# Attention with top-k and two dense layers: a DMA transposes f16 halves of the probabilities, VectorE takes more lower halves

## The chip, the cores and the metric

The kernel runs on one core of a Trainium2 chip, in one launch. The metric is the device time of a run in microseconds (us); lower is better. A core has a matrix engine (TensorE, PE in the profile; its weight loads are PEld), VectorE (DVE), ScalarE (ACT), GpSimd (POOL) and a queue engine (SP) that issues the DMAs here. PSUM is the memory into which PE writes, SBUF the working memory. Each engine takes its instructions in the order in which the program has them.

## The reference

```python
# q, k, v: (4, 8, 576, 64); 8 heads of 64 give 512 columns
scores = (1 / np.sqrt(64)) * np.matmul(q, k.transpose(0, 1, 3, 2))
kth = np.partition(scores, -32, axis=-1)[..., -32:-31]
scores = np.where(scores >= kth, scores, -1e9)
scores = scores - np.max(scores, axis=-1, keepdims=True)
attn = np.exp(scores)
attn = attn / (np.sum(attn, axis=-1, keepdims=True) + 1e-09)
x = np.matmul(attn, v)                       # as rows: (2304, 512)
gate = 1 / (1 + np.exp(-(x @ w_gate)))       # w_gate, w_val: (512, 1536)
h = (gate * (x @ w_val) @ w_out) @ w_in      # w_out: (1536, 512), w_in: (512, 1024)
e = np.exp(h - h.max(-1, keepdims=True))
solu = h * e / (e.sum(-1, keepdims=True) + 1e-9)
ln = (solu - solu.mean(-1)) / np.sqrt(solu.var(-1) + 1e-6) * g_ln
out = ln @ w_out2                            # (1024, 512)
```

## The kernel before

Attention is cut into 72 steps, 18 for each of the four batches. A step has 2 x 128 rows of scores against 576 keys: one pair of heads for 128 queries, or, for the 64 queries left over in each batch, two pairs. The steps 0 to 17 are batch 0 (`WHOLE`, kept in full f32), the others batches 1 to 3. Four steps fill one chunk of 128 rows of `x`; 18 chunks then go through the two dense layers.

A step runs as follows. PE makes the scores (`scores`, L607), ACT copies them to an `s` tile (L614), DVE folds the row's two halves into a `w` tile (L621, L625) and finds the 32 largest with MAX8 and MATCH_REPLACE8 (L635, L639). From the 32nd, DVE and POOL make a threshold (L653 to L663), ACT writes what lies below it to `w` (L668), POOL subtracts that from `s` (L672), ACT takes the exponential with the sum (L677), and DVE inverts the sum (L686). POOL scales the probabilities in place (`norm`, L694; ACT in the first six steps, L692). PE transposes the nine 128 x 128 blocks in three groups (`flip`, L704). For batch 0, ACT copies each group to SBUF (L711). For batches 1 to 3 ACT writes the upper f16 half (`take_flip`, L714), and DVE subtracts it from what PSUM holds and writes the lower half (`rest_flip`, L719). PE multiplies with V (`attend`, L738), for batches 1 to 3 in three f16 products of halves.

The dense layers also work with f16 halves. The upper half is an ACT copy. The lower half is made in one of two ways. In chunks 16 and 17 (`DIRECT`) DVE takes it from PSUM in one instruction (`lower`, L771). In the others ACT makes a second copy in full precision and POOL subtracts: rows of x (`rows_all`, L760, `rows_rest`, L777), the middle (`mid_all`, L948, `mid_rest`, L954), the turned last layer (`turn_all`, L1045, `turn_rest`, L1053).

The order of all this is made before the program is written. `Order` is a planner: each piece of work is added with its engine, a cost, a due time, what it needs, and which tiles it takes and frees. It plays the work forwards and backwards and then writes the instructions in the order found. `SHIFT` holds corrections to the due times, one number for each kind of work. `BUFS` says how many tiles of each kind there are; a tile that is not free holds back the work that takes it. The loads of K land in `s` tiles.

Of the kernel before, what the change touches and what calls it, by code (L numbers as in the profile page):

```python
# [40 lines left out]
DIRECT = (16, 17)
FULL = 2.0 ** 15

BUFS = dict(s=4, ks=8, v=4, qr=3, qs=3, w=2, et=4, eu=2, ps=1, pt=1, av=1, pm=4, xt=1, gh=1, two=3, big=2, xf=1, x2=1)
# [1161 lines left out]
```

## Time and profile before

| | |
|---|---|
| median of 3 runs | 1100.3 us (1100.17 to 1100.45) |
| profiled execution | 1101.9 us |
| its span, first to last instruction | 1100.1 us |
| busy: PE, DVE, ACT, POOL | 970.6, 971.5, 827.8, 701.2 us |
| granted TensorE clock, mean | 0.944 |

The times of engines overlap, so busy times do not add up to the span. The profile shows one execution; "idle before" is the time that an engine stood still just before an instruction, with the one that released it. PE is little used in the first 200 us, while weights are rebuilt and the first steps run; from 200 to 1000 us PE and DVE are nearly full; in the last 100 us PE finishes the last chunks and DVE is at 31%.

### The profile page before, as it was taken

To read this page: it belongs to the slowest core of one execution; us is meant where nothing else is said; L and a number is where in the kernel's file an instruction comes from. 1 tells how busy PE (TensorE), PEld (TensorE's weight loads), DVE (VectorE), ACT (ScalarE), POOL (GpSimd) and SP (SyncE) were. 2 spreads that over 40 slices of the span, in tenths; PEclk is the share of its full clock that TensorE was granted. 3 is DMA by queue.
4 is the path that set the end of the run, shared out by engine and by line. 5 is a ranking of instruction groups with operands and counts; after the bars stand their busy time and mean duration, and the time that the engine had idled before them with its cause. 6 is when DMAs were issued, how large, how long until landed. Compare 5 with 4: busy or idle time off the path is not lost.

```text
span 1100.1 us, 31341 instructions
## 1 busy us (share of the span) xinstructions
PE 970.6 (88%) x12500; PEld 801.8 (73%) x12500; DVE 971.5 (88%) x2888; ACT 827.8 (75%) x1561; POOL 701.2 (64%) x940
## 2 busy tenths in 40 slices
PE   1455747799999999999999999999999999999996
PEld 1334736589796878796978879797878798778952
DVE  7999999999698999999999999997998999893242
ACT  2698499997889787787889677778789787765431
POOL 2556378887877675878678665778678657652100
PEclk9756768899999999999999999999999999999998
DMA  9854241001220000012110000022100000000000
GB/s 318 289 162 139 85 137 69 6 21 52 75 74 12 26 12 22 26 50 64 53 33 7 26 25 8 26 64 63 53 28 22 22 11 7 12 11 11 2 11 19
DMA packets 29474, 59.16 MB, mean 54 GB/s; under 512 B 3984, under 2 KB 14224, under 8 KB 29328
## 3 DMA queue, kind: packets, MB, share of 16 engines
q1 hardware_dynamic: 29328, 57.16, 15.8%
q8 instruction: 98, 1.61, 0.6%
q14 instruction: 48, 0.39, 0.1%
HBM read 52.43 MB, written 4.72 MB: 52 GB/s over the span
## 4 chain that ended last, share of the span: by engine, by line
DVE 32%; PE 31%; ACT 20%; POOL 9%; DMA 5%; issue 3%; POOLq 0%; SPq 0%; DVEq 0%; ACTq 0%
DVE m L635 9%; DVE w L639 7%; PE px L927 6%; PE pg L881 5%; PE ph L964 4%; PE pv L881 4%; PE po L1062 4%; DVE et L719 3%; PE pt L704 3%; ACT w L668 2%; ACT s L677 2%; PE ps L607 2%; POOL s L672 2%; DVE pd L415 2%; DVE pd L411 2%
## 5 line engine op out<-in xcount | busy, mean ns | idle before, releaser
L635 DVE MAX8 m<-w 128x8 f32<-128x576 f32 (+1 forms) x576 | 340.0, 604 | 2.8
L639 DVE MATCH_REPLACE8 w<-m,w 128x288 f32<-128x288 f32 (+1 forms) x432 | 234.9, 545 | 0.0
L672 POOL TENSOR_TENSOR s<-s,w 128x576 f32<-128x576 f32 x144 | 203.2, 1420 | 37.2 <-ACT w L668 36.8
L927 PE MATMUL px<-gh,wo 128*128 128x128 f16 x2592 | 178.4, 220 | 0.0
L881 PE MATMUL pg<-xt,wg 128*128 128x128 f16 x2592 | 168.8, 221 | 8.2 <-POOL xt L777 5.9
L927 PEld LDWEIGHTS <-wo 128*128 128x128 f16 x2592 | 157.3, 98 | 22.3 <-issue 0.5
L881 PE MATMUL pv<-xt,wv 128*128 128x128 f16 x2592 | 168.7, 220 | 0.2 <-ACT xg L948 0.2
L881 PEld LDWEIGHTS <-wv 128*128 128x128 f16 x2592 | 155.3, 99 | 15.6 <-issue 0.7
L881 PEld LDWEIGHTS <-wg 128*128 128x128 f16 x2592 | 154.1, 99 | 14.5 <-issue 6.5
L607 PE MATMUL ps<-ks,qs 128*128 128x288 f32 x640 | 129.2, 330 | 31.4 <-DVE w L625 20.3
L704 PE MATMUL pt<-ident,s 128*128 128x128 f32 x648 | 117.5, 290 | 30.4 <-ACT et L711 14.2
L668 ACT ACTIVATE w<-s,ed 128x576 f32<-128x576 f32 x144 | 120.8, 869 | 25.3 <-POOL ed L663 24.3
L607 PEld LDWEIGHTS ps<-ks,qs 128*128 128x128 f32 x640 | 97.0, 200 | 46.1 <-issue 11.1
L614 ACT ACTIVATE s<-ps 128x576 f32<-128x576 f32 x144 | 93.1, 647 | 43.1 <-PE ps L607 37.4
L677 ACT ACTIVATE s<-s,nm 128x576 f32<-128x576 f32 x144 | 111.7, 776 | 16.8 <-POOL s L672 15.6
L964 PE MATMUL ph<-wi,x 128*128 128x512 f16 x432 | 121.6, 391 | 2.4 <-ACT x L944 2.4
L1062 PE MATMUL po<-wo,lt 128*128 128x512 f16 x432 | 120.5, 394 | 1.6 <-DVE sg L909 1.1
L704 PEld LDWEIGHTS pt<-ident,s 128*128 128x128 f32 x648 | 76.0, 146 | 60.0 <-ACT et L711 20.0
L714 ACT ACTIVATE et<-pt 128x512 f16<-128x512 f32 x162 | 78.9, 487 | 48.1 <-PE pt L704 47.4
L694 POOL TENSOR_SCALAR s<-s,sm 128x576 f32<-128x576 f32 x132 | 97.3, 746 | 21.7 <-DVE sm L686 19.5
L719 DVE SCALAR_TENSOR_TENSOR et<-pt,et 128x512 f16<-128x512 f32 x162 | 89.0, 549 | 18.4 <-ACT et L714 17.8
L738 PE MATMUL av<-et,v 128*64 128x128 f16 (+3 forms) x2200 | 87.0, 234 | 0.2 <-POOL v L597 0.2
(179 smaller groups left out, 1681.4 us busy)
## 6 DMA issues: line engine op xcount, KB each, us to landing
kr<-in_k_dup_dram SPq DMA_DIRECT2D x16, 576.0 KB, 4.0
qr<-in_q_main_dram SPq DMA_DIRECT2D x64, 128.0 KB, 2.4
v<-in_v_pad_dram SPq DMA_DIRECT2D x16, 320.0 KB, 4.0
wi<-in_w_gate_dram SPq DMA_DIRECT2D x8, 512.0 KB, 6.2
wo<-in_w_val_dram SPq DMA_DIRECT2D x8, 512.0 KB, 6.6
raw<-in_w_in_dram SPq DMA_DIRECT2D x8, 512.0 KB, 4.9
wi<-in_w_out_dram SPq DMA_DIRECT2D x8, 512.0 KB, 3.8
raw<-in_w_out_dram SPq DMA_DIRECT2D x8, 512.0 KB, 3.3
```

Source lines behind the costliest of these rows:

```text
L607: nc.tensor.matmul(pt[:, nn, :S // 2], qs[:, hl, slot], ks[:, nn * (S // 2):(nn + 1) * (S // 2)], start=x == 0, stop=x == len(mm) - 1)
L635: nc.vector.max(st["m8"][:, t, r * 8:r * 8 + 8], ranked(i, r, t))
L639: nc.vector.match_replace(w, steps[i]["m8"][:, t, r * 8:r * 8 + 8], w, LOW)
L668: nc.scalar.activation(st["w"][:, t], st["s"][:, t], AF.Relu, bias=st["ed"][:, 1, t:t + 1], scale=st["ed"][:, 0, t:t + 1])
L672: nc.gpsimd.tensor_sub(st["s"][:, t], st["s"][:, t], st["w"][:, t])
L677: nc.scalar.activation(w, w, AF.Exp, bias=st["nm"][:, t:t + 1], scale=D ** -0.5, accum_out=st["sm"][:, t:t + 1])
L704: nc.tensor.transpose(pt[:, x], wf[:, k * P:(k + 1) * P], ident)
L719: nc.vector.scalar_tensor_tensor(et[:, 1], st["pt", g][:, :et.shape[2]], 1.0, et[:, 0], op0=OP.mult, op1=OP.subtract)
L881: nc.tensor.matmul(dst, w[a][:, c, f * P:(f + 1) * P], ch["xt"][:, b, c], start=x == 0, stop=x == len(mm) - 1)
L927: nc.tensor.matmul(ch["px"][:, e], wo1h[a][:, f, e * P:(e + 1) * P], ch["gh"][:, b, f], start=y == 0, stop=y == len(DOWN) - 1)
L964: nc.tensor.matmul(ch["ph", nn], ch["x2"][:, a, c], wih[b][:, c, nn * 512:(nn + 1) * 512], start=c == 0 and a == 0 and b == 0, stop=c == K ...
L1062: nc.tensor.matmul(ch["po"], ch["lt"][:, a, f], wo2h[b][:, f], start=y == 0, stop=y == len(FIN) - 1)
```

## The change

For batches 1 to 3 PE no longer transposes. ACT writes the upper f16 half of the scaled probabilities from `s` into a new tile `h` (`prob_hi`), which takes a `w` tile's place. ACT (first half of the step) and POOL (second half) scale `s` in place as `norm` did, POOL subtracts the upper half and writes the lower (`prob_lo`), and one DMA on SP transposes all 18 blocks of 128 x 128 f16 into an `et` tile (`flip_halves`). `attend` reads that.

`DIRECT` now holds the chunks 4 to 17, so DVE takes the lower halves from PSUM there, with a factor for each half of a chunk that has rows of two batches (`row_factors`). What else chunks 16 and 17 did differently hangs on the new `LATE`. `BUFS` changes: `s` 4 to 3, `w` 2 to 3, `et` and `eu` to two `et` tiles. All numbers of `SHIFT` change, and with them the order; two of its lines are shown.

```diff
-DIRECT = (16, 17)
+DIRECT = tuple(range(4, 18))
+LATE = (16, 17)
-BUFS = dict(s=4, ks=8, v=4, qr=3, qs=3, w=2, et=4, eu=2, ps=1, pt=1, av=1, pm=4, xt=1, gh=1, two=3, big=2, xf=1, x2=1)
+BUFS = dict(s=3, ks=8, v=4, qr=3, qs=3, w=3, et=2, ps=1, pt=1, av=1, pm=4, xt=1, gh=1, two=3, big=2, xf=1, x2=1)
 SHIFT = {
-    ("w", "g"): -488.7, ("sw", "g"): -373.8, ("wl", "g"): -1.3, ("swl", "g"): 331.2, ("w", "v"): -152.2,
...
+    ("M", 7): -116.2, ("M", 8): 264.5, ("M", 9): -207.8, ("M", 10): -5.3, ("M", 11): -98.3, ("M", 12): -78.9,
...
 def norm(i, t):
-        if i < EARLY:
+        if i < EARLY or t == 0 and steps[i]["b"] not in WHOLE:
             nc.scalar.activation(w, w, AF.Copy, scale=st["sm"][:, t:t + 1])
...
+    def prob_hi(i, t):
+        st = steps[i]
+        if "h" not in st:
+            st["h"] = tl(sp, [P, 2, 2, S], F16, f"h{i}", "w")
+        nc.scalar.activation(st["h"][:, 0, t], st["s"][:, t], AF.Copy, scale=st["sm"][:, t:t + 1])
+
+    def prob_lo(i, t):
+        st = steps[i]
+        nc.gpsimd.tensor_sub(st["h"][:, 1, t], st["s"][:, t], st["h"][:, 0, t])
+
+    def flip_halves(i):
+        st = steps[i]
+        st["et"] = tl(sp, [P, 2, NBLK, P], F16, f"et{i}", "et")
+        nc.sync.dma_start(st["et"].rearrange("p c k q -> p (c k) q"), st["h"].rearrange("p c a b -> p (c a b)"), transpose=True)
...
-    def rest_flip(i, g):
-        st = steps[i]
-        et = st["et", g]
-        nc.vector.scalar_tensor_tensor(et[:, 1], st["pt", g][:, :et.shape[2]], 1.0, et[:, 0], op0=OP.mult, op1=OP.subtract)
...
     def rows_direct(ch):
-        lower(ch["xt"][:, 1], ch["av"], 1.0 / PROB, ch["xt"][:, 0])
+        for w, by in row_factors(ch):
+            lower(ch["xt"][:, 1, :, w], ch["av"][:, :, w], by, ch["xt"][:, 0, :, w])
...
+            for t in range(2):
+                add(("hh", i, t), "ACT", 0.67, e, lambda i=i, t=t: prob_hi(i, t), [("iv", i)] + [("hh", i, 0)] * t, take=["w"] * (t == 0))
+                add(("no", i, t), *(("ACT", 0.67) if t == 0 else ("POOL", 0.73)), e, lambda i=i, t=t: norm(i, t), [("hh", i, t)])
+                add(("hl", i, t), "POOL", 1.385, e, lambda i=i, t=t: prob_lo(i, t), [("no", i, t)] + [("hl", i, 0)] * t,
+                    free=["s"] * t)
+            add(("tr", i), "DMA", 3.5, e + 3, lambda i=i: flip_halves(i), [("hl", i, 1)], take=["et"], free=["w"], delay=1.5)
```

In the changed kernel the lines are 1 to 17 higher: the folds are L622 and L626, MAX8 L636, `norm` L693 and L695, `prob_hi` L717, `prob_lo` L721, `flip_halves` L726, `lower` L782, the first matrices' products L898, the threshold's penalty L673. The names below carry the number of the step behind the tile's letter (`w42` is the `w` tile of step 42, `m8` its 8 x 4 maxima with the step behind, `et41_0` the first group of step 41).

On DVE, in the middle of batch 2, before: the top-k work of steps 43 and 44, with lower halves of the steps 40 and 41.

```order
L719 SCALAR_TENSOR_TENSOR et40_2_10362<-pt40_2_10346,et40_2_10362 128x128
L977 TENSOR_REDUCE st_10344<-st_10344 128x1
L635 MAX m843_10173<-w43_10128 128x8
L980 TENSOR_SCALAR st_10344<-st_10344,n2_9518 128x1
L621 TENSOR_TENSOR w44_10393<-ps44_0_10365,s44_10385 128x288
L639 MATCH_REPLACE w43_10128<-m843_10173,w43_10128 128x576
L625 TENSOR_TENSOR w44_10393<-ps44_0_10365,s44_10385 128x288
L635 MAX m843_10173<-w43_10128 128x8
L996 TENSOR_SCALAR st_10344<-st_10344 128x1
L686 RECIPROCAL sm42_10158<-sm42_10158 128x2
L719 SCALAR_TENSOR_TENSOR et41_0_10419<-pt41_0_10387,et41_0_10419 128x512
```

The same place now, at the start of step 42:

```order
L782 SCALAR_TENSOR_TENSOR lt_9533<-pl_9478,lt_9533 128x512
L636 MAX m841_9438<-w41_9427 128x8
L782 SCALAR_TENSOR_TENSOR x2_9552<-px_8856,n2_9393,x2_9552 128x512
L622 TENSOR_TENSOR w42_9616<-ps42_0_9556,s42_9595 128x288
L640 MATCH_REPLACE w41_9427<-m841_9438,w41_9427 128x576
L636 MAX m842_9626<-w42_9616 128x8
L636 MAX m841_9438<-w41_9427 128x8
L640 MATCH_REPLACE w42_9616<-m842_9626,w42_9616 128x288
L782 SCALAR_TENSOR_TENSOR lt_9533<-pl_9599,lt_9533 128x512
```

The three lower halves of a step are gone; lower halves of the dense layers stand between the top-k instructions instead, four to a chunk of four steps.

On POOL, at step 42, before: subtraction, scaling, and the rows of chunk 9.

```order
L672 TENSOR_TENSOR s42_9936<-s42_9936,w42_9950 128x576
L645 TENSOR_SCALAR nm43_10304<-m843_10173 128x2
L672 TENSOR_TENSOR s42_9936<-s42_9936,w42_9950 128x576
L777 TENSOR_TENSOR xt9_10295<-xf_10309,xt9_10295 128x512
L682 TENSOR_SCALAR sm42_10158<-sm42_10158 128x2
L694 TENSOR_SCALAR s42_9936<-s42_9936,sm42_10158 128x576 x2
```

POOL at step 42 now:

```order
L673 TENSOR_TENSOR s42_9595<-s42_9595,w42_9616 128x576
L565 TENSOR_TENSOR qs46_0_9833<-qr46_0_9549,qs46_0_9833 128x256
L683 TENSOR_SCALAR sm42_9778<-sm42_9778 128x2
L663 TENSOR_TENSOR ed44_9943<-m844_9804,ed44_9943 128x2
L664 TENSOR_SCALAR ed44_9943<-ed44_9943 128x2
L673 TENSOR_TENSOR s44_9771<-s44_9771,w44_9786 128x576
L721 TENSOR_TENSOR h42_10016<-s42_9595,h42_10016 128x576
L646 TENSOR_SCALAR nm43_10105<-m843_10020 128x2
L695 TENSOR_SCALAR s42_9595<-s42_9595,sm42_9778 128x576
L673 TENSOR_TENSOR s44_9771<-s44_9771,w44_9786 128x576
L721 TENSOR_TENSOR h42_10016<-s42_9595,h42_10016 128x576
```

One scaling is gone from POOL and two subtractions (L721) have come, with the penalty of step 44 between them; the rows of the chunk are gone.

On SP, at the boundary to batch 2 (`kr2` are the loads of K of that batch), now:

```order
L726 DMA_TRANSPOSE et30_7249<-h30_7070 128x18x128
L569 DMA kr2_0_7334<-in_k_dup_dram 128x2x576
L555 DMA qr38_0_7376<-in_q_main_dram 128x256
L726 DMA_TRANSPOSE et31_7544<-h31_7339 128x18x128
L569 DMA kr2_1_7602<-in_k_dup_dram 128x2x576
L555 DMA qr39_0_7712<-in_q_main_dram 128x256
L569 DMA kr2_2_7797<-in_k_dup_dram 128x2x576
L726 DMA_TRANSPOSE et32_7819<-h32_7673 128x18x128
```

The transposing DMAs stand in one queue with the loads, one to a step; before, the queue held loads and stores alone. On PE, behind the last product of attention, there stand 51 products of the last layer (72 before), 228 of the third matrix (204), 16 transposes (24); the numbers of the other products are the same.

## Rows read from the trace of the kernel before

**Rows 1.** The page: busy time by engine, and the chain that ended last
```profile
PE 970.6 (88%) x12500; PEld 801.8 (73%) x12500; DVE 971.5 (88%) x2888; ACT 827.8 (75%) x1561; POOL 701.2 (64%) x940
...
DVE 32%; PE 31%; ACT 20%; POOL 9%; DMA 5%; issue 3%; POOLq 0%; SPq 0%; DVEq 0%; ACTq 0%
```

**Rows 2.** Busy time by stretch: start:end, length, engines, granted clock, DMA share, GB/s
```profile
200.00:300.00 100.00, 95.66 (x1165) 80.84 (x1164) 91.58 (x284) 85.83 (x164) 82.16 (x110) 0.98 0.13 38
300.00:400.00 100.00, 95.57 (x1396) 82.23 (x1394) 93.17 (x300) 87.76 (x174) 75.23 (x103) 1.00 0.11 36
...
300.00:992.00 692.00, 676.26 (x9345) 567.16 (x9343) 659.75 (x2039) 554.42 (x1081) 492.42 (x681) 1.00 0.10 31
```

**Rows 3.** The chain, 300 to 992 us, longest pieces: start, length, what
```profile
488.35 4.70 DMA kr<-in_k_dup_dram
...
736.91 3.73 DMA kr<-in_k_dup_dram
```

**Rows 4.** Groups of DVE, 300 to 992 us: busy, mean ns, idle before
```profile
L719 DVE SCALAR_TENSOR_TENSOR et<-pt,et 128x512 f16<-128x512 f32 x103 | 70.2, 681 | 6.9 <-ACT et L714 6.7
...
L719 DVE SCALAR_TENSOR_TENSOR et<-pt,et 128x128 f16<-128x128 f32 x51 | 14.5, 284 | 0.4 <-ACT et L714 0.2
```

**Rows 5.** One piece of the chain (0.60), and the timeline of DVE
```profile
614.50 0.60 DVE et L719
...
599.34 0.27 DVE L719 SCALAR_TENSOR_TENSOR et<-pt,et 128x128 f16<-128x128 f32 x1
599.53 0.14 DVE L653 TENSOR_SCALAR ed<-m 128x1 uint32<-128x1 uint32 x1
```

**Rows 6.** Timeline of PE's weight side: the transposes of one step
```profile
601.07 0.42 PEld L704 LDWEIGHTS pt<-ident,s 128*128 128x128 f32 x4
...
604.55 0.42 PEld L704 LDWEIGHTS pt<-ident,s 128*128 128x128 f32 x4
...
607.44 0.14 PEld L704 LDWEIGHTS pt<-ident,s 128*128 128x128 f32 x1
```

**Rows 7.** Groups of ACT over the whole span, by shape
```profile
L714 ACT ACTIVATE et<-pt 128x512 f16<-128x512 f32 x108 | 64.1, 593 | 39.5 <-PE pt L704 39.2
...
L1045 ACT ACTIVATE lf<-pl 128x512 f32<-128x512 f32 x32 | 19.3, 604 | 0.2 <-POOL lt L1053 0.2
...
L714 ACT ACTIVATE et<-pt 128x128 f16<-128x128 f32 x54 | 14.8, 275 | 8.6 <-PE pt L704 8.2
...
L948 ACT ACTIVATE xg<-px,n 128x512 f32<-128x512 f32 x16 | 11.2, 698 | 0.0
...
L692 ACT ACTIVATE s<-s,sm 128x576 f32<-128x576 f32 x12 | 8.7, 764 | 1.6 <-DVE sm L686 1.5
```

**Rows 8.** Groups of POOL over the whole span, by shape
```profile
L672 POOL TENSOR_TENSOR s<-s,w 128x576 f32<-128x576 f32 x144 | 203.2, 1420 | 37.2 <-ACT w L668 36.8
...
L694 POOL TENSOR_SCALAR s<-s,sm 128x576 f32<-128x576 f32 x132 | 97.3, 746 | 21.7 <-DVE sm L686 19.5 <-DVE ed L657 1.3 <-DVE ed L653 0.2
...
L915 POOL TENSOR_TENSOR gh<-sg,gh 128x512 f16<-128x512 f32 x48 | 55.7, 1162 | 15.0 <-ACT gh L912 14.3
...
L1053 POOL TENSOR_TENSOR lt<-lf,lt 128x512 f16<-128x512 f32 x32 | 37.3, 1165 | 13.0 <-ACT lf L1045 12.8
```

**Rows 9.** DMA issues: how many, KB each, median us to landing
```profile
kr<-in_k_dup_dram SPq DMA_DIRECT2D x16, 576.0 KB, 4.0
...
gl<-in_g_ln_dram SPq DMA_DIRECT2D x1, 4.0 KB, 4.5
```

**Rows 10.** Timeline of step 42: first fold into `w`, last subtraction
```profile
599.59 0.45 DVE L621 TENSOR_TENSOR w<-ps,s 128x288 f32<-128x288 f32 x1
...
617.59 1.42 POOL L672 TENSOR_TENSOR s<-s,w 128x576 f32<-128x576 f32 x1
```

**Rows 11.** A piece of the chain after 992 us
```profile
1059.94 0.68 PE po L1062 x3
```

More of the change, by code (lines that the diff above doesn't have):

```diff
@@ L161, in terms @@
     own += [((k, "first"), 1.0)] * (name[1] < 18) + [((k, "end"), 1.0)] * (name[1] > 63)
-    return [((k, name[2]) if k in ("m", "r", "fl", "et", "ez") else k, 1.0), (("A", name[1] // 4), 1.0)] + own
+    return [((k, name[2]) if k in ("m", "r", "fl", "et") else k, 1.0), (("A", name[1] // 4), 1.0)] + own
 class Order:
@@ L174 @@
                 POOL=(100, 70, 80, 100, 1250), DMA=(0,) * 5)
-    TAKER = dict(s="ACT", ks="POOL", v="DMA", qr="DMA", qs="POOL", w="DVE", et="ACT", eu="ACT", ps="PE", pt="PE", av="PE", pm="PE",
+    TAKER = dict(s="ACT", ks="POOL", v="DMA", qr="DMA", qs="POOL", w="DVE", et="ACT", ps="PE", pt="PE", av="PE", pm="PE",
                  xt="ACT", gh="ACT", two="ACT", big="DMA", xf="ACT", x2="ACT")
@@ L773, in rows_direct @@
     def rows_direct(ch):
-        lower(ch["xt"][:, 1], ch["av"], 1.0 / PROB, ch["xt"][:, 0])
+        for w, by in row_factors(ch):
+            lower(ch["xt"][:, 1, :, w], ch["av"][:, :, w], by, ch["xt"][:, 0, :, w])
     def rows_rest(ch):
@@ L836, in body @@
         add(("iv", i), "DVE", 0.08, e, lambda i=i: inverse(i), [("iw", i)])
-        for t in range(2):
-            add(("no", i, t), *(("ACT", 0.67) if i < EARLY else ("POOL", 0.73)), e, lambda i=i, t=t: norm(i, t), [("iv", i)])
-        for g in range(3):
-            add(("fl", i, g), "PE", (0.45, 0.45, 0.13)[g], e + 6, lambda i=i, g=g: flip(i, g),
-                [("no", i, 0), ("no", i, 1)] + [("fl", i, x) for x in range(2) if g == 2], take=["pt"],
-                free=["s"] if g == 2 else [])
-            add(("et", i, g), "ACT", (0.49, 0.49, 0.17)[g], e + 6, lambda i=i, g=g: take_flip(i, g), [("fl", i, g)] + [("et", i, g - 1)] * (g > 0),
-                take=(["et"] * 2, [], ["eu"])[g],
-                free=["pt"] * (b in WHOLE))
-            if b not in WHOLE:
-                add(("ez", i, g), "DVE", (0.6, 0.6, 0.2)[g], e + 6, lambda i=i, g=g: rest_flip(i, g), [("et", i, g)], free=["pt"])
@@ L848, in body @@
-        whole = b in WHOLE
-        needs = [("et" if whole else "ez", i, x) for x in range(3)]
+        whole = b in WHOLE
+        if whole:
+            for t in range(2):
+                add(("no", i, t), *(("ACT", 0.67) if i < EARLY else ("POOL", 0.73)), e, lambda i=i, t=t: norm(i, t), [("iv", i)])
+            for g in range(3):
+                add(("fl", i, g), "PE", (0.45, 0.45, 0.13)[g], e + 6, lambda i=i, g=g: flip(i, g),
+                    [("no", i, 0), ("no", i, 1)] + [("fl", i, x) for x in range(2) if g == 2], take=["pt"],
+                    free=["s"] if g == 2 else [])
+                add(("et", i, g), "ACT", (0.49, 0.49, 0.17)[g], e + 6, lambda i=i, g=g: take_flip(i, g),
+                    [("fl", i, g)] + [("et", i, g - 1)] * (g > 0), take=["et"] * (g == 0), free=["pt"])
+        else:
+            for t in range(2):
+                add(("hh", i, t), "ACT", 0.67, e, lambda i=i, t=t: prob_hi(i, t), [("iv", i)] + [("hh", i, 0)] * t, take=["w"] * (t == 0))
[3 more added lines that the diff above has]
+            add(("tr", i), "DMA", 3.5, e + 3, lambda i=i: flip_halves(i), [("hl", i, 1)], take=["et"], free=["w"], delay=1.5)
@@ L850, in body @@
+        needs = [("et", i, x) for x in range(3)] if whole else [("tr", i)]
         needs += [n for p in st["pairs"] for n in ([("vd", b, p)] if whole else [("vl", b, p, x) for x in range(2)])]
@@ L853, in body @@
             take=["av"] if st["first"] else [],
-            free=list(ET) + ["v"] * sum(uses[b, p][-1] == i for p in st["pairs"]))
+            free=["et"] + ["v"] * sum(uses[b, p][-1] == i for p in st["pairs"]))
         if st["last"]:
@@ L870, in body @@
             if ch["x"] in DIRECT:
-                add(("xl", ch["x"]), "DVE", 0.6, e + 6, lambda ch=ch: rows_direct(ch), [("xh", ch["x"])], free=["av"])
+                add(("xl", ch["x"]), "DVE", 0.6 if len(ch["vs"]) == 1 else 0.75, e + 6, lambda ch=ch: rows_direct(ch), [("xh", ch["x"])], free=["av"])
             else:
@@ L1026, in ln4 @@
         st = ch["st"]
-        if ch["x"] in DIRECT:
+        if ch["x"] in LATE:
             nc.vector.tensor_scalar(ch["e"], ch["e"], st[:, 8:9], st[:, 9:10], op0=OP.add, op1=OP.mult)
@@ L1104, in body @@
             op(("gi", f), "ACT", 0.52, a, lambda ch=ch, f=f: gated_hi(ch, f), [("gt", x, f)])
-            op(("gl", f), *(("DVE", 0.6) if x in DIRECT else ("POOL", 1.12)), a, lambda ch=ch, f=f: gated_lo(ch, f), [("gi", x, f)], free=["two"],
+            op(("gl", f), *(("DVE", 0.6) if x in LATE else ("POOL", 1.12)), a, lambda ch=ch, f=f: gated_lo(ch, f), [("gi", x, f)], free=["two"],
                port=True)
```

28 lines of the change are left out of this document (13 added, 15 removed), and 141 rows, old and new, of the table SHIFT.

## The prediction

> **What bounds the kernel now.** I read the page's busy shares first: PE and DVE are both at 88% of the span, ACT at 75%, POOL at 64%, and the chain that ended last is shared by DVE (32%) and PE (31%) [rows 1]. So neither engine alone is the bound, and the next view is the stretches. The one from 300 to 992 us holds the top-k work of the 54 steps of batches 1 to 3, that is 692 / 54 = 12.81 us a step. There PE is busy 676.3 us (97.7%) and DVE 659.8 (95.3%), at a granted clock of 1.00; ACT has 554.4 and POOL 492.4 [rows 2]. What shortens a step must therefore take time from PE and from DVE together. After 992 PE alone works off the last chunks. At two batch boundaries the loads of K stand in the chain [rows 3]: they borrow an `s` tile, so tiles are short there already.
>
> **The change part by part.** The profiled execution took 1101.9 us, its span 1100.1; the median of the runs is 1100.3. I make the sum as a difference of span and take it from 1100.3.
>
> *DVE.* In each of 54 steps three lower-half instructions go, two of 512 and one of 128 elements. Their means are 681 and 284 ns, but they overlap with the neighbours [rows 4]: in the chain a large one takes 0.60, and from the start of the small one at 599.34 the next begins at 599.53, 0.19 [rows 5]. That is 2 x 0.60 + 0.2 = 1.4 us a step, 75.6 in all. New are the lower halves of chunks 4 to 15: 24 in the turn of the last layer, 12 in the middle, 10 full and 4 half ones of the rows, the same kind of instruction: 46 x 0.60 + 4 x 0.33 = 28.9. Net -46.7. In DVE's order 3.6 us of what goes and 1.2 of what comes stand behind the last top-k instruction, so the path to it becomes 44 us shorter. DVE also stood 6.9 + 0.4 us idle before these instructions, waiting for ACT's upper halves [rows 4]; what is late next is usually a MAX8 whose data lie ready. The 50 new ones wait for an ACT upper half too, at the same 0.05 us each 2.3 in all. -5.
>
> *PE.* 486 of the 648 transposes go. Four take the weight side 0.42 us and the ninth 0.14 [rows 6], so 0.98 us a step, 53 in all, a little more than DVE gains. I take these slots, not the products' own times, which overlap with the neighbours. PE therefore does not keep DVE from its 49, and I count no gain for PE on its own.
>
> *ACT.* New: 108 upper halves from SBUF and 54 scalings of the first half, by the nearest row 764 ns each: 123.8. Gone: 108 and 54 evictions (64.1 + 14.8), and the full-precision copies, 14 of the rows and 24 of the turn at about 604 ns and 12 of the middle at 698 (31.3) [rows 7]. Net about +14: (554.4 + 14) / 54 = 10.5 us a step.
>
> *POOL.* New: 108 subtractions of 576 elements. The f16 row of 512 gives 1162 x 576 / 512 = 1.31, the f32 row of 576 gives 1.42: 141 to 153 us. Gone: 54 scalings at 746 ns (40.3) and 48 subtractions of 512 at 1165 (55.9) [rows 8]. Net +45 to +57; I take 51, which makes 543 us or 10.1 a step. This hides behind DVE's and PE's 12 us only as long as the order keeps POOL's waits short.
>
> *The transposing DMA.* It moves 128 x 2304 x 2 bytes, 576 KB, 54 times, and nothing in the trace does that. The plain load of the same 576 KB lands after 4.0 us: the lower end. For the upper end, `gl` moves 1024 separate 4-byte words in 4.5 us [rows 9], at most 4.4 ns a piece; the block is 2304 pieces of 128 elements, 10.1 us. I take 5.5, nearer to the row with the same bytes. (Moved as 294,912 single elements it would be 1.3 ms each; I give that under 1 in 100 and leave it out.) While it runs no engine works on it, and attention waits for it in place of three hops PE, ACT, DVE; its cover is that a step is attended some three steps after its scores, in the order before as now. Behind it on SP's queue stand loads of q and K and the stores, issued well ahead.
>
> [...]
>
> *Tiles.* `w` goes from two to three and now also holds the f16 halves until the DMA has read them; `s` goes from four to three and is held longer, until the last subtraction. In one step `w` is held from 599.59 to 617.59 + 1.42 = 619.01, 19.4 us [rows 10]. The halves add 0.76 + 0.76 (ACT) + 1.42 + 0.75 + 1.42 (POOL) = 5.1, about 1 for handovers (estimate), and the DMA's 5.5: 11.6. Together 31.0 of three tiles' 3 x 12.1 = 36.3. It fits with 5 us to spare, less where a K load holds one of three `s` tiles. For that, and for the fuller POOL and ACT, I add 10 us of new waits: the three boundaries at the length of one K load each (3.7 to 4.7, [rows 3]) give 12, none gives 0.
>
> *The tail.* Behind the last attention product PE's order now has 51 products of the last layer instead of 72, 228 instead of 204 of the third matrix and 16 instead of 24 transposes. Three of 512 columns take 0.68 [rows 11], 12 of 128 have as many columns: -21 x 0.227 + 24 x 0.057 - 8 x 0.105 = -4.
>
> Sum: -44 - 5 + 10 - 4 = -43, and 1100.3 - 43 = **1057 us**. The first 300 us I leave as they are: as much DVE work stands ahead of the first step of batches 1 to 3 as before.
>
> **The rivals.** *First, POOL sets the pace.* It gets 51 us and stands in the path of every step three times. For: the rise from 492 to 543 us in a stretch of some 650 would be 83%, and its fullest 100 us so far had 82.2 [rows 2]. Against: the fullest stretch of ACT was 87.8, so in-order engines can be that full. At 82% the stretch would last 543 / 0.82 = 662 us, 30 less than 692, with the tail 1066; at 79% 687, and 1091. I take 1078.
>
> *Second, the tiles run out and it is slower.* Price and point: a step lasts at least (19.4 + 6.1 + DMA) / 3, so from 12.9 us between issue and release on it is over today's 12.81. The DMA could get there at its upper bound of 10.1 with 5 more on SP's queue, behind a K load that waits for an `s` tile: 15.1 gives 13.5 us a step, 54 x 0.72 = +39, with the tail 1135. For: three `s` tiles instead of four, and K loads that are in the chain with four. Against: the same bytes land in 4.0 us as a plain load, and DMA is busy 0.10 of that stretch [rows 2].
>
> *Third, hidden anyway:* PE's and DVE's releases are given back to a longer latency of each step, within 2 us of 1100.
>
> **How the numbers follow.** Forecast (1038 to 1072) 0.58; POOL's pace (1066 to 1091) 0.18; a larger gain, under 1038, where the 10 us of new waits don't come and other idle time of DVE shrinks too, 0.04; no change (within 0.2%, which is about what a measurement can tell) 0.05; slower by the tiles 0.15. So faster 0.80, same 0.05, slower 0.15. The range leaves out the slow case and most of the largest gain: 1036 to 1100.
>
> **What would show it.** Right: between the first and last top-k of batches 1 to 3 some 650 us instead of 692; DVE's busy sum down by about 47 to 56, PE's by at least 53; L726 landing in 4 to 7 us; idle time before L717 and L721 small. Wrong: DVE idle before L622 with a DMA or POOL as releaser (tiles), POOL over 85% busy, or L726 over 10 us. If the stretch is shorter and the end isn't, the tail was mis-read.

## The result, and the profile after

The changed kernel takes 1091.3 us at the median (1087.0 to 1091.9), the kernel before in the same series 1100.4. The ratio is 0.9903, with a 95% interval of 0.9874 to 0.9933: faster, by about 9 us. The forecast was 43 us, so the direction was right and four fifths of the gain did not come. The profiled execution has a span of 1089.6 us.

The page's busy times and its chain, of the kernel after; they answer to [rows 1]:

```profile
PE 923.2 (85%) x12014; PEld 757.9 (70%) x12014; DVE 927.1 (85%) x2776; ACT 842.7 (77%) x1511; POOL 744.3 (68%) x946
...
PE 21%; DVE 11%; ACT 9%; POOL 8%; DMA 3%; issue 2%; POOLq 0%; ACTq 0%; DVEq 0%
```

The work went as forecast: VectorE (DVE) has 44 us less, TensorE (PE) 47, ScalarE (ACT) has 15 more, GpSimd (POOL) 43 more. The chain can't be set beside the one before share by share: it is traced back only to about 500 us, so its shares add up to some 54% of the span. Of that traced part PE has 39%, DVE 20%, ACT 17% and POOL 15%, where PE and DVE had 31% and 32% of a chain traced over the whole span. DVE's part has fallen, and the chain is a mixture of short pieces of every engine.

Next, the stretches from the first top-k of step 18 to the last top-k, and from there to the end: start:end, length, busy us of PE, PEld, DVE, ACT and POOL, granted clock, DMA share, GB/s. First before, cut at the same two events as after, then after.

```profile
302.90:992.10 689.20, 674.59 (x9331) 566.23 (x9330) 659.11 (x2038) 551.62 (x1078) 489.52 (x678) 1.00 0.10 30
992.10:1100.10 108.00, 95.47 (x1117) 69.84 (x1114) 32.69 (x79) 38.97 (x70) 13.39 (x21) 0.95 0.03 11
```

```profile
298.40:993.50 695.10, 653.67 (x9046) 540.38 (x9045) 624.56 (x1947) 575.79 (x1045) 533.67 (x688) 0.98 0.37 74
993.50:1089.60 96.10, 79.99 (x993) 61.38 (x990) 26.31 (x62) 33.54 (x55) 13.97 (x21) 0.94 0.14 28
```

These four rows hold the result. The stretch of 54 steps is 5.9 us longer, 12.87 us a step where it was 12.76. DVE's work in it fell by 34.6 us (659.1 to 624.6), but its idle time, length less busy, rose by 40.4 (30.1 to 70.5). ("Idle" below is always that difference.) The 9 or 10 us that were gained lie at the two ends: the stretch starts 4.5 us earlier, and after the last top-k PE has 15.5 us less to work off and ends 11.9 us sooner. Sum: -4.5 - 34.6 + 40.4 - 11.9 = -10.6, the 10.5 between the spans. These are single executions, and the control e1 below, with the same instructions and as many tiles, has 689.5 us in the stretch: what is shown is that the stretch did not get shorter, not that it got longer.

What DVE waits for in that stretch (line, tile and releaser: us, times, longest), before and after:

```profile
DVE w L621 <- ACT s L614: 9.8, 10, 3.4
DVE et L719 <- ACT et L714: 6.9, 8, 2.8
DVE sm L686 <- POOL sm L682: 4.1, 5, 2.9
DVE st L996 <- ACT e L988: 2.5, 2, 1.7
```

```profile
DVE w L622 <- ACT s L615: 18.1, 15, 4.8
DVE w L622 <- DMA et<-h: 11.4, 9, 2.7
DVE lt L782 <- ACT lt L1058: 9.8, 5, 2.6
DVE sm L687 <- POOL sm L683: 5.3, 9, 1.4
DVE w L622 <- POOL s L673: 4.5, 2, 3.9
DVE st L1013 <- ACT e L1005: 3.9, 5, 1.2
DVE w L622 <- ACT junk L1033: 2.2, 1, 2.2
```

The wait at `et` L719 is gone. In its place DVE waits at L622, the first fold of a step's scores into `w`, with three kinds of releaser: ACT has not yet copied the scores, the transposing DMA still reads the `w` tile that holds float16 halves, POOL has not yet let `w` go. Those three are 34.0 us, against 9.8.

When ACT copies the scores late, that is mostly because they came late from PE, and not because no `s` tile was free. The waits of ACT's copy and of PE's scores, in the same stretches, before and after:

```profile
ACT s L614 <- PE ps L607: 19.0, 16, 3.8
PE ps L607 <- DVE w L625: 1.1, 4, 0.4
```

```profile
ACT s L615 <- PE ps L608: 25.3, 21, 3.9
ACT s L615 <- POOL h L721: 3.3, 3, 2.1
PE ps L608 <- DVE w L626: 9.9, 10, 3.7
```

The scores have one `ps` tile in PSUM (`ps=1` in `BUFS`), so PE makes the next ones only when DVE's second fold has read the last ones. The waits in that ring from DVE over PE and ACT back to DVE have grown too, and no run gave it a second tile.

The groups of the new work (busy us, mean ns, idle before), and the landing times:

```profile
L721 POOL TENSOR_TENSOR h<-s,h 128x576 f16<-128x576 f32 x108 | 139.2, 1289 | 45.2 <-ACT s L693 11.0 <-DVE r L752 7.2 <-DVE w L622 7.2
...
L717 ACT ACTIVATE h<-s,sm 128x576 f16<-128x576 f32 x108 | 82.7, 769 | 17.4 <-DVE sm L687 11.9 <-DVE ed L654 4.9 <-DVE ed L658 0.3
```

```profile
kr<-in_k_dup_dram SPq DMA_DIRECT2D x16, 576.0 KB, 4.1
...
et<-h SPq DMA_TRANSPOSE x54, 5.0
```

Durations are near the forecast: 1.29 us against 1.31 to 1.42, 0.77 against 0.76, 5.0 against 5.5. Sizes of instructions are not what failed. Nor is SP's queue, for the most part: by the trace 46 of the 54 transposing DMAs are issued within 0.2 us of the end of POOL's last lower half; the other 8 come 0.5 to 6.9 us late, 22 us together.

Last, one step followed through the timelines of ACT, DVE, POOL and SP (start, length, instruction): step 42's scores into `s`, first fold, second subtraction on `w`, first upper half, last lower half, the DMA.

```profile
602.01 0.65 ACT L615 ACTIVATE s<-ps 128x576 f32<-128x576 f32 x1 [0.99 <-PE ps L608]
...
602.70 0.46 DVE L622 TENSOR_TENSOR w<-ps,s 128x288 f32<-128x288 f32 x1 [0.52 <-ACT s L615]
...
622.51 1.42 POOL L673 TENSOR_TENSOR s<-s,w 128x576 f32<-128x576 f32 x1
...
627.84 0.76 ACT L717 ACTIVATE h<-s,sm 128x576 f16<-128x576 f32 x1
...
634.21 1.29 POOL L721 TENSOR_TENSOR h<-s,h 128x576 f16<-128x576 f32 x1
...
635.52 2.68 SPq L726 DMA_TRANSPOSE et<-h  x1
```

The step holds an `s` tile for 33.5 us (602.01 to 635.50; the mean of the 54 steps is the same), a `w` tile for 21.2 as scores and for some 13 as halves, until the DMA has landed. At 12.87 us a step, 33.5 us of three `s` tiles' 38.6 are taken before any K load borrows one, so 2.6 steps are under way at a time.

### The profile page after: what moved, and what is told of

The parts are those of the page before. It is cut to its first block, busy times and chain, and to the rows that moved or that the text cites. A ratio compares the mean times of both kernels' runs of the same rounds, so it can differ in the third digit from the quotient of the medians.

```text
span 1089.6 us, 30410 instructions
## 1 busy us (share of the span) xinstructions
PE 923.2 (85%) x12014; PEld 757.9 (70%) x12014; DVE 927.1 (85%) x2776; ACT 842.7 (77%) x1511; POOL 744.3 (68%) x946
## 4 chain that ended last, share of the span: by engine, by line
PE 21%; DVE 11%; ACT 9%; POOL 8%; DMA 3%; issue 2%; POOLq 0%; ACTq 0%; DVEq 0%
PE pv L898 4%; DVE m L636 4%; PE po L1079 3%; PE px L944 3%; PE pg L898 3%; PE ph L981 3%; DVE w L640 3%; POOL h L721 2%; PE ps L608 2%; DMA kr<-in_k_dup_dram 1%; DMA et<-h 1%; ACT w L669 1%; PE av L745 1%; POOL ks L578 1%; POOL s L673 1%
## 5 line engine op out<-in xcount | busy, mean ns | idle before, releaser
L636 DVE MAX8 m<-w 128x8 f32<-128x288 f32 (+1 forms) x576 | 337.0, 601 | 2.5
L673 POOL TENSOR_TENSOR s<-s,w 128x576 f32<-128x576 f32 x144 | 203.8, 1421 | 31.3 <-ACT w L669 30.7
L944 PE MATMUL px<-gh,wo 128*128 128x128 f16 x2592 | 175.1, 219 | 1.4 <-POOL gh L932 1.4
L608 PE MATMUL ps<-ks,qs 128*128 128x288 f32 x640 | 131.9, 335 | 51.4 <-DVE w L626 38.0
L944 PEld LDWEIGHTS <-wo 128*128 128x128 f16 x2592 | 154.9, 98 | 27.5 <-issue 2.0
L898 PE MATMUL pg<-xt,wg 128*128 128x128 f16 x2592 | 170.3, 224 | 2.3 <-DVE xt L782 1.3
L898 PE MATMUL pv<-xt,wv 128*128 128x128 f16 x2592 | 168.9, 223 | 3.5 <-ACT sg L923 3.3
L898 PEld LDWEIGHTS <-wv 128*128 128x128 f16 x2592 | 157.0, 100 | 19.4 <-issue 4.4
L721 POOL TENSOR_TENSOR h<-s,h 128x576 f16<-128x576 f32 x108 | 139.2, 1289 | 45.2 <-ACT s L693 11.0
L898 PEld LDWEIGHTS <-wg 128*128 128x128 f16 x2592 | 156.6, 101 | 8.9 <-issue 3.1
L608 PEld LDWEIGHTS ps<-ks,qs 128*128 128x128 f32 x640 | 99.1, 203 | 73.4 <-issue 15.5
L622 DVE TENSOR_TENSOR w<-ps,s 128x288 f32<-128x288 f32 x144 | 64.6, 449 | 49.6 <-ACT s L615 29.0
L717 ACT ACTIVATE h<-s,sm 128x576 f16<-128x576 f32 x108 | 82.7, 769 | 17.4 <-DVE sm L687 11.9
L565 POOL TENSOR_TENSOR qs<-qr,qs 128x256 fp32r<-128x256 f32 x80 | 58.7, 735 | 48.2 <-ACT qs L561 46.9
L695 POOL TENSOR_SCALAR s<-s,sm 128x576 f32<-128x576 f32 x78 | 58.3, 749 | 10.0 <-DVE ed L654 4.0
```

Of the source, the lines that this page charges most:

```text
L608: nc.tensor.matmul(pt[:, nn, :S // 2], qs[:, hl, slot], ks[:, nn * (S // 2):(nn + 1) * (S // 2)], start=x == 0, stop=x == len(mm) - 1)
L636: nc.vector.max(st["m8"][:, t, r * 8:r * 8 + 8], ranked(i, r, t))
L673: nc.gpsimd.tensor_sub(st["s"][:, t], st["s"][:, t], st["w"][:, t])
L721: nc.gpsimd.tensor_sub(st["h"][:, 1, t], st["s"][:, t], st["h"][:, 0, t])
L898: nc.tensor.matmul(dst, w[a][:, c, f * P:(f + 1) * P], ch["xt"][:, b, c], start=x == 0, stop=x == len(mm) - 1)
L944: nc.tensor.matmul(ch["px"][:, e], wo1h[a][:, f, e * P:(e + 1) * P], ch["gh"][:, b, f], start=y == 0, stop=y == len(DOWN) - 1)
```

## The experiments

Two measures are given: the median time, with the ratio to the kernel before on the same chip, and the stretch from the first top-k of step 18 to the last one, with DVE's idle time in it. The medians of the kernel before lie between 1098.8 and 1100.4 in all series, so times can be set side by side; the runs of one kernel spread over 2 to 10 us, so a difference of under 4 us is not told from none.

| run | us | ratio, 95% interval | stretch | DVE idle |
|---|---|---|---|---|
| changed kernel | 1091.3 | 0.9903 (0.9874-0.9933) | 695.1 | 70.5 |
| e1 control, 3 `s`, 3 `w` | 1088.9 | 0.9915 (0.9896-0.9935) | 689.5 | 65.0 |
| e2 4 `s` | 1078.8 | 0.9821 (0.9807-0.9836) | 685.2 | 61.3 |
| e3 4 `w` | 1083.9 | 0.9864 (0.9849-0.9879) | 686.4 | 62.6 |
| e4 4 `s`, 4 `w` | 1074.7 | 0.9790 (0.9774-0.9807) | 680.0 | 56.6 |
| e5 DMA doubled | 1211.0 | 1.1021 (1.0990-1.1051) | 805.1 | 178.8 |
| e6 POOL -53 us | 1085.2 | 0.9881 (0.9842-0.9920) | 685.4 | 61.3 |
| e7 DVE's dense halves out | 1088.5 | 0.9909 (0.9885-0.9934) | 692.0 | 91.8 |
| e8 no scaling | 1073.5 | 0.9763 (0.9738-0.9788) | 676.9 | 52.8 |
| e9 PE -30 us | 1089.7 | 0.9909 (0.9879-0.9938) | 695.1 | 70.4 |
| e10 e4 and e8 | 1065.0 | 0.9696 (0.9680-0.9712) | 670.0 | 47.2 |
| e11 e4 and e9 | 1077.3 | 0.9800 (0.9783-0.9817) | 679.9 | 56.5 |
| e12 lower half on DVE | 1107.1 | 1.0071 (1.0056-1.0086) | 710.5 | 43.6 |
| e13 e4 and e5 | 1152.0 | 1.0484 (1.0447-1.0521) | 745.2 | 119.7 |
| e14 half landed | 1083.2 | 0.9855 (0.9835-0.9875) | 687.0 | 62.9 |
| e15 two DMAs of half | 1082.5 | 0.9852 (0.9823-0.9881) | 684.8 | 60.2 |
| e16 e10 and e15 | 1065.7 | 0.9686 (0.9662-0.9709) | 671.1 | 47.7 |
| e17 e16 and e7 | 1061.1 | 0.9651 (0.9629-0.9672) | 665.9 | 67.1 |
| e18 e15, scaling on ACT | 1095.0 | 0.9955 (0.9939-0.9971) | 697.9 | 73.2 |

Three theories stood at the start. T1: the tiles `s` and `w` run out and set the step. T2: the chain over ScalarE and GpSimd, in each engine's fixed order, sets it. T3: VectorE's own order sets it, with the dense layers' lower halves that wait for ScalarE. A fourth, T4, came with e9: TensorE's own work sets it. All kernels keep the changed kernel's issue order, but for what they take out, put in at the same place, or move to another engine there.

**More tiles (e1 to e4).**

```diff
-        return pool.tile(shape, dtype, name=name, tag=tag, bufs=bufs or BUFS[tag])
+        return pool.tile(shape, dtype, name=name, tag=tag, bufs=bufs or dict(BUFS, s=4, w=3)[tag])
...
-    wv = cp.tile([P, KD, FF1], F32, name="wv")
+    wv = cp.tile([P, KD, FF1 - 512], F32, name="wv")
+    wx = cp.tile([P, 512], F32, name="wx")
+    wy = cp.tile([P, 512], F16, name="wy")
```

This is e2; e1 has s=3 and w=3, e3 s=3 and w=4, e4 four of both and scratch for the gate matrix too.

> The control for the three that follow. Left out: the last 512 of the value matrix's 1536 columns have no place of their own; their float32 words and lower halves are kept in two scratch tiles that every later piece overwrites, and the products of those columns read the columns of the first 512. Every instruction of the changed kernel is still issued, in the same order on each engine; the number of tiles is the same: three for s, three for w. Every theory expects the changed kernel's time, 1091 us, within 5 us, and the same 12.9 us per step between the first top-k of step 18 and the last one. A difference beyond that would be the price of the scratch tiles in the loading stage, before step 18.

> The control with a fourth tile for s (the raw scores, later the probabilities), every instruction in the same order. After the change, an s tile is held for 33.5 us of a step's life on average, with 12 more that hold a K piece for about 14 us; of three tiles that is about 95% of the 12.87 us per step. Theory T1 (the tiles set the step): the waits of VectorE's eviction of the scores for s and w, 38 us in the stretch of steps 18 to 71, shrink to under 20, and the time falls by 15 to 35 us against the control. Theory T2 (the in-order chain over GpSimd and ScalarE sets the step): the waits move from the s tile to the next link, and the time falls by 6 us at most. Theory T3 (VectorE's own order, with its lower halves of the dense layers that wait for ScalarE, 20.7 us): as T2, within 6 us.

> The control with a fourth tile for w (copies of the scores that the top-k eats, then the transposed halves' float16 tile in the same memory), three for s. A w tile is taken by a step for 20.3 us as scores and 10.3 us as the halves before and during the transposing DMA, 30.6 us of 38.6: 79% of three tiles. T1, if w is the tile that binds: the eviction's 11.4 us of waits for the transposing DMA and part of those for ScalarE go, 10 to 25 us faster than the control. T1, if s is the one: under 5 us. T2 and T3: under 5 us.

> Four tiles for s and four for w, the same order. Left out: as in the control, but for the last 512 columns of the gate matrix as well. T1: at least the larger of the two gains before, 20 to 45 us faster than the control; the eviction waits for no tile at all. T2: 8 us at most, and the idle time of VectorE, 70 us in the stretch, stays above 55 with other releasers (GpSimd's lower halves, ScalarE's transposes). T3: the same, with ScalarE's lt tile as the releaser that grows.

Measured: the control is at the changed kernel's time. Against it a fourth `s` gives 10 us, a fourth `w` 5, both 14. So tiles cost something, and `s` more than `w`, but 14 us is under what T1 asked for (20 to 45), and 56.6 us of DVE's idle time stay, with no wait at the fold for an `s` or `w` tile:

```profile
DVE w L626 <- ACT s L619: 16.4, 16, 4.7
DVE sm L691 <- POOL sm L687: 11.8, 10, 4.6
DVE lt L786 <- ACT lt L1062: 10.1, 5, 2.6
```

In these rows of e4 (DVE's waits in its stretch) the DMA and POOL no longer stand among the releasers of the fold; that the scores come late does. T1 is a part, not the whole.

**The DMA doubled (e5), and doubled with four tiles (e13).**

```diff
-        nc.sync.dma_start(st["et"].rearrange("p c k q -> p (c k) q"), st["h"].rearrange("p c a b -> p (c a b)"), transpose=True)
+        for _ in range(2):
+            nc.sync.dma_start(st["et"].rearrange("p c k q -> p (c k) q"), st["h"].rearrange("p c a b -> p (c a b)"), transpose=True)
```

> The changed kernel with the transposing DMA issued twice in each of the 54 steps, the second writing the same tile again; nothing else is touched. One landed in 5.0 us at the median, so the halves' tile (the memory of a w tile) is held some 3 to 5 us longer per step, and the product of the probabilities and V may start that much later. T1 (tiles set the step): with w held 34 to 36 us of 38.6 instead of 30.6, the waits of the scores' eviction grow by a good part of 54 x 3 us: 20 to 50 us slower than the changed kernel. T2 and T3 (in-order chains over GpSimd, ScalarE and VectorE): the transposes are off the path, 0 to 8 us slower. The fourth w tile gave 5 us back, which speaks for a price of some 5 to 20.

> The transposing DMA issued twice per step, as in e5, with four tiles for s and for w (the last 512 columns of the gate and value matrices share scratch, as in e4). Ring of tiles: a fourth tile carries 5 us more of holding (3 x 12.6 = 38 us are held of 4 x 12.6 = 50), so it costs 0 to 25 us over the 1074.7 us of e4. Chain: the products wait for the second landing in TensorE's fixed order, tiles or not, 80 to 130 us over e4.

Measured: +120 us over the changed kernel, more than any theory gave, and with four tiles still +77 over e4 (1074.7 to 1152.0), just under the 80 to 130 of the chain and far over the 25 of the tiles. Of the 120, then, 43 hung on the number of tiles and 77 did not. Where those 77 lie, PE's waits in e13's stretch show:

```profile
PE av L750 <- DMA et<-h: 52.3, 19, 5.1
PE ps L612 <- DVE w L630: 8.3, 7, 3.2
```

The attention products wait for the second landing, and in PE's fixed order the next scores stand behind them. In e5 the fold's waits are 44.5 us for the DMA (13 times) and 45.5 for ACT's scores. Loads stand behind the second DMA in SP's queue too, and ACT's wait for K is longer as well (7.1 us in the changed kernel, 17.3 in e13 between 298 and 975 us): not all of the price is the step's own. TensorE's granted clock fell too, as the rows of e5's and e13's stretches show:

```profile
298.90:1104.00 805.10, 683.59 (x9054) 563.98 (x9052) 626.28 (x1947) 578.18 (x1045) 533.80 (x687) 0.93 0.52 101
```

```profile
296.90:1042.10 745.20, 662.95 (x9057) 550.47 (x9055) 625.50 (x1947) 577.41 (x1045) 534.03 (x688) 0.95 0.58 109
```

PE stood idle in between, and the mean granted clock is 0.93 and 0.95 against 0.98: the same 9,050 matmuls or so take 683.6 us in e5, 653.7 in the changed kernel. So a delay in a step's path shows twice, as waiting and as a slower PE; how much of the 120 us is the second, no run separates.

**Work off one engine (e6, e7, e9, e11).** In turn GpSimd's lower half of the gate's product, VectorE's lower halves of the dense rows, and one partial product on TensorE:

```diff
-        (nc.vector if ch["x"] in LATE else nc.gpsimd).tensor_sub(ch["gh"][:, 1, f:f + 4], ch["sg", f], ch["gh"][:, 0, f:f + 4])
+        if ch["x"] in LATE:
+            nc.vector.tensor_sub(ch["gh"][:, 1, f:f + 4], ch["sg", f], ch["gh"][:, 0, f:f + 4])
...
-        lower(lo, ch["pl", nn], 1.0, hi)
+        if ch["x"] in LATE:
+            lower(lo, ch["pl", nn], 1.0, hi)
...
             f, a, b = DOWN[y]
+            if a == 1 and ch["x"] not in LATE:
+                continue
```

> GpSimd's lower half of the gate's product left out in chunks 0 to 15 (48 instructions of 1.165 us, 56 us of its 744); the product with the first output matrix reads the upper halves twice in their place, so TensorE does the same work. Left out is therefore the lower half of that product. T2, GpSimd sets the pace: 20 to 50 us faster than the changed kernel. T1 and T3: the lower halves of the probabilities, which GpSimd makes and on which the s tile's end hangs, come a little earlier: 0 to 10 us faster.

> VectorE's lower halves of rows from PSUM left out in chunks 4 to 15 (some 29 us of work that VectorE has taken from GpSimd and ScalarE, and 20.7 us of waiting before them for the upper halves of ScalarE); the products read the upper half twice. Left out is the lower half of these rows. T3: the waiting goes too, 35 to 50 us faster than the changed kernel. T1: the work is gone, but the tiles still hold the step: VectorE waits at the eviction of the scores for what it no longer waits elsewhere, 0 to 15 us faster. T2: 0 to 10 us.

> One of the three partial products of the gated rows with the second gate's output matrix left out in chunks 0 to 15 (the lower half of the matrix by the upper half of the rows): 768 matmuls of 128 columns, about 52 us of TensorE's 923 at 67.6 ns each. Nothing else is changed, so that product lacks this part. A new theory, T4: TensorE, 94% busy from the first top-k of step 18 to the last one, is the bound that took over, and its own work sets the step: 30 to 50 us faster than the changed kernel. T1 (tiles) and T2 (the chain over ScalarE and GpSimd that lets the tiles go): TensorE waits for VectorE and the DMA, and with less work it waits more: 0 to 10 us faster, most of it behind the last top-k, where TensorE alone works off two chunks.

> Four tiles for s and for w, and the partial product of e9 left out. If TensorE is the bound once the tiles are not (95% busy in the stretch there), 25 to 45 us faster than the 1074.7 us of four and four. If the step is set by the chain through ScalarE, GpSimd and VectorE, under 12 us faster.

Measured: 6, 3 and 2 us, and none in e11 (1077.3 against 1074.7). PE's busy time fell by 30 us (923.2 to 892.9), not by the 52 of the expectation. The amount of work of POOL, DVE or PE alone doesn't set the step; ACT's was not varied by itself, and no run took work from DVE and PE together. T3 falls, and so does T4. How the time is given back is plain in e7, DVE's waits and its stretch:

```profile
DVE w L622 <- ACT s L615: 31.0, 27, 4.6
DVE sm L687 <- POOL sm L683: 9.1, 14, 1.4
```

```profile
297.70:989.70 692.00, 652.35 (x9044) 539.28 (x9044) 600.25 (x1899) 576.38 (x1045) 533.75 (x688) 0.98 0.37 74
```

DVE has 24.3 us less to do in the stretch and idles 21.2 us more; the wait for ACT's copy of the scores rises from 18.1 to 31.0, while that copy waits for PE as long as before (25.9 us). That is, in small, what the change itself did.

**Shorter steps (e8, e10).**

```diff
         w = st["s"][:, t]
+        if st["b"] not in WHOLE:
+            return
         if i < EARLY or t == 0 and steps[i]["b"] not in WHOLE:
```

> The probabilities' in-place scaling by the inverse of their sum left out in batches 1 to 3: 54 instructions of 0.77 us on ScalarE and 54 of 0.75 us on GpSimd go, and the s tile is let go some 2.3 us earlier per step. Left out is that scaling in these batches. T1: the s tile's hold falls from 33.5 to 31 us; with what the fourth s tile gave (10 us) as the most that a tile can give, 5 to 12 us faster than the changed kernel. T2: 41 us off ScalarE and 41 off GpSimd in the chain that the step waits for: 15 to 40 us faster.

> The two changes that gave most, together: four tiles for s and for w (14 us by themselves) and the in-place scaling of the probabilities left out (18 us), with what each leaves out. T1: they work on the same thing, the time for which a tile is held against the number of tiles, so the gains do not add: 1066 to 1073 us. T2: the scaling's gain is in the work of ScalarE and GpSimd, not in the tiles, so the gains add: 1054 to 1064 us.

Measured: e8 gains 18 us with 34 us off ACT's busy time and 39 off POOL's, work that stands inside a step, between the sum of the exponentials and the lower halves. 53 us off POOL in a dense layer (e6) gave 6; there is no such counterpart for ACT. With four tiles it is 26 us in all, against 32 if the two gains added, and 1065.0 falls between the two theories' ranges. Tiles and path work largely on the same thing, not quite.

**The lower half on VectorE (e12).**

```diff
         w = st["s"][:, t]
+        if t == 0 and st["b"] not in WHOLE:
+            return
...
-        nc.gpsimd.tensor_sub(st["h"][:, 1, t], st["s"][:, t], st["h"][:, 0, t])
+        if t == 0:
+            nc.vector.scalar_tensor_tensor(st["h"][:, 1, t], st["s"][:, t], st["sm"][:, t:t + 1], st["h"][:, 0, t],
+                                           op0=OP.mult, op1=OP.subtract)
+        else:
+            nc.gpsimd.tensor_sub(st["h"][:, 1, t], st["s"][:, t], st["h"][:, 0, t])
```

> A version that computes the reference: the lower half of the first 128 rows of a step's probabilities is made by VectorE, in one instruction that multiplies by the inverse sum and subtracts the upper half, where GpSimd subtracted; their in-place scaling on ScalarE goes. Per step -0.77 us on ScalarE, -1.29 on GpSimd, about +0.66 on VectorE (36 us in all, estimate from the 0.60 us of 512 elements), every other instruction in the same order. T1 and T2: the s tile is let go earlier and ScalarE and GpSimd have less, as in the run without scaling, 8 to 20 us faster than the changed kernel; VectorE has 70 us of idle time in the stretch and pays at most a few us of it back. If VectorE still is what bounds the step: 10 to 36 us slower.

Measured: 16 us slower, a miss. One such instruction took 0.81 us, not 0.66, 44 us in all, and DVE's stretch reads

```profile
298.40:1008.90 710.50, 653.21 (x9062) 537.10 (x9060) 666.93 (x2000) 544.36 (x994) 484.88 (x638) 0.98 0.35 72
```

DVE is busy 94% again. Its idle time fell by 27 us to 43.6, so DVE's slack could be filled only in part, and the rest came out as time, though ACT and POOL had 80 us less in the stretch. Slack in waits for the next scores was no free room for work inside the step.

**A shorter landing (e14, e15), all together (e16, e17), and e18.** e15's edit:

```diff
-        nc.sync.dma_start(st["et"].rearrange("p c k q -> p (c k) q"), st["h"].rearrange("p c a b -> p (c a b)"), transpose=True)
+        for c in range(2):
+            nc.sync.dma_start(st["et"][:, c], st["h"][:, c].rearrange("p a b -> p (a b)"), transpose=True)
```

e14 runs that loop for c = 0 alone. e16 is e4, e8 and e15 together, e17 that and e7. e18 is e15 with the condition `i < EARLY or steps[i]["b"] not in WHOLE` for ScalarE in `norm`.

> The transposing DMA moves the upper halves alone, 288 KB in place of 576, issued at the same place; the products read the upper half twice. Left out are the lower halves of the probabilities in batches 1 to 3. GpSimd still makes them and the DMA still comes after them in SyncE's order, but need not wait for them. If it lands 1.5 to 2 us sooner and the price of e5 (120 us for 54 x 5 us, 0.44 us per us) holds below 5 us too: 35 us faster than the changed kernel; if it also starts before GpSimd's last lower half, more. If the price is one of running over an edge (tiles that just suffice): 0 to 12 us faster.

> A version that computes the reference: two transposing DMAs of 288 KB per step, first the upper halves, then the lower, in place of one of 576 KB. The first needs only ScalarE's upper halves, which are there some 3 us before GpSimd's last lower half, so the second alone is behind GpSimd and lands 1 to 2 us sooner than one of 576 KB. Chain with an even price: 20 to 40 us faster than the changed kernel. Edge: 0 to 10 us faster. If two issues one behind the other cost more than they save (a second fixed price of some 2 us, as the 2.0 us of the smallest store shows): up to 30 us slower.

> Four tiles for s and for w, the scaling of the probabilities left out in batches 1 to 3, and the halves landed by two transposing DMAs as in e15 (left out: what e10 leaves out). If the landing's 9 us are a part of what tiles and scaling give (one chain, one price): 1060 to 1066 us against e10's 1065. If they are a wait of their own: 1053 to 1059 us, which is the forecast's 1057 and would account for all of the missing 34 us.

> e16 without VectorE's lower halves of the dense rows in chunks 4 to 15, as in e7 (left out: those lower halves too). If VectorE sets the step once the holds are short, as the forecast took it: 12 to 25 us faster than e16. If the fixed order and TensorE (96% busy in e10's stretch) hold it: 0 to 6 us, as in e7.

> A version that computes the reference: e15, and the in-place scaling of the second 128 rows moved from GpSimd (0.75 us) to ScalarE (0.77 us), where it runs beside GpSimd's first lower half. The halves are ready up to 0.75 us sooner. If GpSimd's row of three is what holds the s tile: 3 to 10 us faster than e15. If ScalarE (576 of 688 us in the stretch) is as late: 0 to 8 us slower.

Measured: e14 and e15 both gain 8 to 9 us. In e15 a landing of 288 KB takes 3.4 us, and DVE's wait for the DMA falls from 11.4 to

```profile
DVE w L622 <- DMA et<-h: 3.6, 5, 1.4
```

The first of the two DMAs starts before POOL's last lower half, the second lands 1.6 us sooner than one of 576 KB. (The 2.0 us in e15's expectation is the landing of the 256 KB stores; the smallest ones, of 128 KB, took 2.8.) That the gain is 9 and not 35 says that the price of e5 does not hold downwards: above 5 us each us of landing costs 24 (120 / 5.0), below it 5 or 6 (9 / 1.6). In e14 the one DMA does not wait for the lower halves at all: by the trace it has landed 0.6 us after the last of them (median), where the changed kernel has 5.3 and e15 3.9, and yet e14 gains no more than e15. So what a landing gives back soon comes to an end. On top of e10 the split gives nothing (1065.7 against 1065.0), so its 9 us are a part of the same 26. e16's stretch:

```profile
297.40:968.50 671.10, 644.36 (x9046) 533.88 (x9044) 623.39 (x1946) 542.02 (x993) 495.78 (x637) 0.99 0.40 77
```

PE is busy 96%, DVE 93%. Taking 24.6 us off DVE there (e17) gives 4.5 to 5 us, not the 12 to 25 of a bound; PE's work was not reduced there. e18 is 12 us slower than e15, beyond the 8 that were expected at most: ACT's busy time in the stretch goes from 576 to 608 us, the fold's wait for ACT's scores from 18.7 to 24 us; moving this work from POOL to ACT within a step is no relief.

e15 leaves nothing out and is the fastest such kernel, 1.5% under the kernel before. The changed kernel's interval and e15's overlap a little (0.9874 to 0.9933 and 0.9823 to 0.9881), so that it also beats the change by 9 us is likely, not shown.

## Why the prediction was wrong

*What bounds the kernel.* Right as a reading, PE and DVE 98% and 95% busy [rows 2]; wrong in what followed from it. Both lost time together, as the text asked for, and the step did not get shorter.

*DVE, -44 and -5.* The work term was near: 44.4 us less in all, where 46.7 were worked out, but 38 of them ahead of the last top-k instead of 44 (34.6 in the stretch and 3.5 before it). The step that failed is the sentence behind it, that what is late next is usually a MAX8 whose data lie ready. Next late is the fold into `w`, whose scores, `s` tile and `w` tile all come out of the pipeline of the steps before. e7 shows it: 24.3 us less for DVE, 21.2 us more waiting, and the waits at that fold go from 38.3 to 59.6 us. The 50 new lower halves that were to wait 2.3 us waited 11.3 in the stretch (`lt` and `x`), but without them (e7) nothing came back.

*PE, ACT, POOL.* The amounts were right (-47 against -53, +15 against +14, +43 against +45 to +57). That PE would not keep DVE from its gain holds for PE's amount of work (e9 and e11 moved nothing); that its scores come late in its fixed order was not in the sum.

*The DMA.* 5.0 us against 5.5, inside its bounds; the plain load of the same bytes landed in 4.1. What the time of landing is worth was mis-sized: it was weighed only as a part of a tile's holding. The transposing DMA took 0.9 us more than that plain load, which comes from DRAM and not from SBUF.

*Tiles, +10.* This is the term of the sum that was mis-sized: DVE's idle time rose by 40.4 us in the stretch. `w` came out near the forecast (by the trace a mean of 32.8 us in a step, 31.0 were forecast), but the tile that is fuller, `s`, was not worked out at all: 33.5 us in each of 54 steps and 12 K loads of some 14 us are 1977 us of 3 x 695, 95%. Full tiles alone are still only 14 us of it (e4). The larger part is, as far as these runs go, the path of a step: from scores to landed halves it now has ACT, POOL twice over, and a DMA in place of PE, ACT and DVE, while 2.6 steps fit into the three tiles and the fixed order. What lengthens it inside lengthens the step time (e5, e13), what shortens it gives some back (e8, e15), and work outside it counts for little (e6, e7, e9). Relieving both, e10, brings 26 of the missing 34 us, though it leaves out the scaling that the forecast had counted.

*The tail, -4.* Where it was worked out, behind the last attention product, it was right: from the start of that product to the end there were 75.3 us (1024.8 to 1100.1) and are now 69.7 (1019.9 to 1089.6), 5.6 less. Another 6.3 us came off between the last top-k and that product, 32.7 to 26.4, and 4.5 at the start, which the sum left as they were. That the time fell at all is due to these ends, not to the step for which the change was made; so the right direction is in part luck.

*The rivals.* POOL at 77% of the stretch (533.7 of 695.1) is not the pace (e6), though the 1091 that was worked out for 79% is the time that was measured, which is luck. The tiles running out had the right place (L622 with DMA and POOL as releasers) and too high a price. The third, releases given back to a longer latency of each step, had a chance of 0.05, and within the stretch it is what happened (689.2 us before, 695.1 after, 689.5 in the control).

*What stays open.* Some 8 us between e16 and the forecast, and more where it was to come from: some 650 us were forecast for the stretch, e16 has 671.1, and the ends hide the rest. There PE and DVE are 96% and 93% busy; DVE does not set the step alone (e17), for PE this was tested in e11 only. The change also brought another issue order, which no run varied by itself, and the scores kept their one `ps` tile; whether another order with the same work, or a second such tile, would close it is not known.
